# Transposing the normalised A of six batches by DMA instead of on TensorE, and E's way through DRAM on SP's queue

## The chip, the cores and the metric

One of the eight cores of a Trainium2 chip runs the program. TensorE multiplies matrices (PE; its weight loads are shown as PEld), VectorE (DVE), ScalarE (ACT) and GpSimd (POOL) do the rest of the arithmetic, and SyncE (SP) issues DMAs. Each engine runs its own list of instructions in order and waits on semaphores for the others. The metric is the time of one execution on the device in microseconds.

## What is computed

A Nyström attention (8 batches, 8 heads, 576 positions, 64 per head, 32 landmarks) feeds a multiplicative feed-forward layer:

```python
q_lm = q.reshape(B, H, m, S // m, D).mean(axis=3)       # m = 32 landmarks of 18 rows
k_lm = k.reshape(B, H, m, S // m, D).mean(axis=3)
A  = softmax(scale * q @ k_lm^T)                         # 576 x 32 per head
Bm = softmax(scale * q_lm @ k_lm^T)                      # 32 x 32
C  = softmax(scale * q_lm @ k^T)                         # 32 x 576
Z  = Bm^T / (norm_1(Bm) * norm_inf(Bm) + 1e-6)
for _ in range(6):
    Z = 2 * Z - Z @ Bm @ Z
x = (A @ Z @ C @ v), heads put side by side              # 4608 x 512
out = ((x @ w1) * (x @ w2) @ w3) @ w_out                 # 4608 x 512
```

## The kernel before

Nothing is multiplied in the order written above. `w3 @ w_out` is made once at the start (`w34`, the w3 rows j = 0 to 7, each in two f16 parts of the weights). Four heads of one batch are a quad: there are 16 quads, n = 0 to 15, and quad n belongs to batch n // 2. For each quad the landmarks' means are taken (on PE for the first `NE` quads, on POOL for the others), the scores S and A are multiplied (`s_mm`, `a_mm`), and softmaxes are taken. The exponentials of C, named E, have to be turned so that positions lie on partitions: for the first `NT` = 4 quads by PE, for later ones by DVE in 32x32 blocks (`ecx`), a write to DRAM (`edr`, one DMA a batch, `e_out`) and eight reads back (`ecT`, `e_move`). Then C v is multiplied (`cv_mm`, tasks C0 to C7), the inverse Z is iterated for two batches at a time, and Z C v is folded into w1 and w2 (`W`, then `U`, whose results are `u`).

A's softmax, normalised, is written by POOL to `ah` (`a_norm`, L744). PE turns it in blocks of 128x128 (`a_trans`, L753): four blocks a quad, and a fifth for the odd quads that holds the last two rows of each landmark for both quads. ACT copies the blocks from PSUM into `aT` (`a_copy`, L763 for the four, L766 for the fifth) and sorts the columns as it does so. `aT` is the moving operand of `d1_mm`, which makes both halves of the feed-forward layer in tiles of 192 positions; ACT copies one half out (`asb`, L1097), DVE multiplies it by the other into `ab` (L1103), and `d2_mm` multiplies `ab` with `w34`. ACT scales the result into `osb` (L1129), and SP stores it (`d2_store`, L1144) in the order of rows that `aT`'s columns stand for.

The order of each engine's list is made before anything runs, by a planner in the file (`Plan`). Every task is added with an engine, a duration, the tasks it depends on, the buffers it takes and gives back, and a priority (a due time); the planner plays the program through with these and writes the instructions in the order it found. On PE the constants `MP`, `MT` and `MY` favour staying in the same kind of matmul (full array, or one of several tilings). DMAs are issued in the planned order too: the loads of q and k, of w1 and w2, and the six writes and 48 reads of E from POOL, everything else from SP (the last three stores partly from ACT). A DMA on a queue in this program waits for the one eight places earlier.

In the code nearly all matmuls go through one helper, so they have one line, L296, and are told apart by the tiles that they write and read.

Of the kernel before, what the change touches and what calls it, by code (L numbers as in the profile page):

```python
# [15 lines left out]
S = 576  # L16
# [3 lines left out]
GRP = S // M  # L20
# [1 line left out]
DM = 512  # L22
DF = 1024
HALF = 288
MP = 1.8
MT = 6.0
MY = 0.0
GR = int(2.0)
THIRD = 192
NCH = 8  # L30
# [3 lines left out]
NV = 4  # L34
# [179 lines left out]
def kernel(  # L214
# [93 lines left out]
    def dense(b):  # L308
        return T0 + PER * b
# [7 lines left out]
        return max(12.0 + 6.0 * n, first)  # L317

    def lane(g):
        return dense(GROUPS[g][0]) - 22.0  # L320

    def cvt(b):
        g, i = GOF[b]
        return lane(g) - 10.0 + 3.0 * (i + 2 - len(GROUPS[g]))

    LQ = int(1.0)
    NT = 2 * int(2.0)
    NE = int(2.0)
    L0 = 3.0
    UO = 2.0  # L330
    GO = 10.0


    def const_a():
# [133 lines left out]
                                 scale=1.0 / (WSC * WSC))  # L468
        return fn

    W1 = 2.0
    JS = int(4.0)
    JH = 3.0
    PWL = [(), (3,), (1, 4), (1, 3, 5), (1, 3, 5, 7)][int(2.0)]
    PEB = int(2.0)
    FIRST = [(0, 1), (1, 4), (4, 8)] if PEB else [(0, 4), (4, 8)]

    def w34_tasks():
        for j in range(8):
            p0 = 4.0 + 7.7 * j  # L480
            add(f"w3n{j}", "SP", 0.43 if j < PEB else 1.7, load_w3(j), acq=[("w3n", f"w3n{j}", 1, 3 if j == 0 and PEB else 2)],
                prio=-0.01 if j == 0 else 0.1 + 0.01 * W1 - 0.005 if j == 1 else p0 - 7.0,
                after=0.0 if j < 2 else max(0.0, p0 - 7.0 - 4.0), parts=1 if j < PEB else 4, move=1.42 if j < PEB else 1.8,
                lat=1.9, share=3.75 if j < PEB else 2.85)
            if j == 0:
                for c in range(8):
                    if c % 2 == 0:
                        add(f"wf{c}", "SP", 1.72, load_wout(c), prio=0.1 + 0.01 * c, parts=4, move=1.55, lat=1.9, share=1.92)
                    add(f"woh{c}", "ACT", 0.53, wout_hi(c), deps=[f"wf{c - c % 2}"],
                        prio=1.0 + 0.1 * c)  # L490
                    if c in PWL:
                        add(f"ws{c}", "ACT", 0.53, wout_scale(c), deps=[f"wf{c - c % 2}", f"woh{c}"], prio=1.05 + 0.1 * c)
                        add(f"wol{c}", "POOL", 1.05, wout_sub(c), deps=[f"ws{c}"], prio=-1.0 + 0.1 * c)
                    else:
                        add(f"wol{c}", "DVE", 0.62, wout_lo(c), deps=[f"wf{c - c % 2}", f"woh{c}"],
                             prio=1.0 + 0.1 * c)
            cuts = FIRST if j == 0 else [(0, 4), (4, 8)]
            for h, (c0, c1) in enumerate(cuts):
                k = (c1 - c0) / 4
                deps = [f"w3n{j}"] + ([f"wt{j}{h - 1}"] if h else [])  # L500
                pe = j < PEB
                add(f"wt{j}{h}", "PE" if pe else "DVE", 0.86 * k + 0.03 if pe else 0.64,
                    (w3_ptr if pe else lambda j, h, c0, c1: w3_tr(j, h))(j, h, c0, c1), deps=deps + ["cb"],
                    acq=[("P", f"ptr{j}{h}", 1, 2)], rel=[f"w3n{j}"], prio=p0 - 4.0 + h, mode="128x32" if pe else None)
                add(f"wh{j}{h}", "ACT", 0.13 + 0.35 * k, w3_hi(j, h, c0, c1), deps=[f"wt{j}{h}"] + ([f"wh{j}0"] if h else []),
                    acq=[] if h else [(f"w3t{W3S[j]}", f"w3t{j}", 1, 8)] + ([(f"vb{W3S[j]}", f"wv{j}", 1, 1)] if W3S[j] > 1 else []), rel=[f"ptr{j}{h}"], prio=p0 - 3.5 + h)
                add(f"wl{j}{h}", "DVE", 0.1 + 0.5 * k, w3_lo(j, h, c0, c1), deps=[f"wh{j}{h}"], rel=[f"ptr{j}{h}"],
                    prio=p0 - 3.5 + h)
            part = {c: h for h, (c0, c1) in enumerate(cuts) for c in range(c0, c1)}
            for c in range(8):  # L510
                last = [f"wv{j}"] if c == 7 and W3S[j] > 1 else []
                hi, lo = [f"woh{c}", f"wh{j}{part[c]}"], [f"wol{c}", f"wl{j}{part[c]}"]
                bank1 = [("P", f"pw{j}", 1, 1)] if c == 0 else []
                if j < JS:
                    add(f"mh{j}{c}", "PE", 0.22, w34_mm(j, c, 0), deps=hi + ([f"mh{j}{c - 1}"] if c else []),
                        acq=bank1, prio=p0 + 0.7 * c - JH, mode="full")
                    add(f"mm{j}{c}", "PE", 0.435, w34_mm(j, c, 1), deps=lo + [f"mh{j}{c}"] + ([f"mm{j}{c - 1}"] if c else []),
                        rel=[f"w3t{j}"] + last, prio=p0 + 0.7 * c, mode="full")
                    continue
                add(f"mm{j}{c}", "PE", 0.65, w34_mm(j, c), deps=hi + lo + ([f"mm{j}{c - 1}"] if c else []),  # L520
                    acq=bank1, rel=[f"w3t{j}"] + last, prio=p0 + 0.7 * c, mode="full")
            add(f"wo{j}", "ACT", 0.48, w34_out(j), deps=[f"mm{j}7"], rel=[f"pw{j}"], prio=p0 + 6.0)
# [168 lines left out]
    def a_mm(n):  # L691
        def fn():
            T, lm, ps, o = Tqs[at(f"Tq{n}")], lmTs[at(f"lmT{n}")], a_bank(n), 4 if n % 2 else 2
            for i in range(4):
                for e in range(2):
                    mm(ps[:, 128 * i:128 * i + 128], T[:, o + 4 * i:o + 4 * i + 4, :, e], lm[:, 4:8, :, e],
                       start=(e == 0), stop=(e == 1))
        return fn

# [41 lines left out]
    def a_norm(n):  # L741
# [4 lines left out]
                in1=tinies[at(f"ta{n}")][:, 0:g].unsqueeze(2).to_broadcast([128, g, M]), op=ALU.mult)  # L746
        return fn

    def a_trans(n):
        def fn():  # L750
            ps = bank(at(f"pT{n}")).bitcast(FP16)
            for i in range(a_cols(n) // 128):
                nc.tensor.transpose(  # L753
                    out=ps[:, 128 * i:128 * i + 128],
                    in_=ahs[at(f"ah{n}")][:, 4 * i:4 * i + 4, :].rearrange("p g m -> p (g m)"),
                    identity=ident16[:, :])
        return fn

    def a_copy(n):
        def fn():  # L760
            b, qd = divmod(n, 2)
            ps, t = bank(at(f"pT{n}")).bitcast(FP16), aTs[at(f"aT{b}")]
            nc.scalar.copy(out=t[:, qd, 0:512].rearrange("p (i l r) -> p i l r", i=4, r=4),  # L763
                           in_=ps[:, 0:512].rearrange("p (i r l) -> p i l r", i=4, r=4))
            if qd:
                nc.scalar.copy(out=t[:, :, 512:S].rearrange("p a (l r) -> p a l r", r=2),  # L766
                               in_=ps[:, 512:640].rearrange("p (a r l) -> p a l r", a=2, r=2))
        return fn

    def quad_tasks(n):  # L770
# [2 lines left out]
        add(f"lq{n}", "POOL", 1.2, load_qk(n), acq=[("nat", f"nat{n}", 1, 3)],  # L773
            prio=p - (16.0 if n < 4 else 20.0),
            after=max(L0, p - (20.0 if n < 4 else 20.0)), parts=2, move=3.3, lat=1.83, share=4.46)
        add(f"lv{n}", "SP", 1.72, load_v(n), acq=[(f"vb{n % NV}", f"vb{n}", 1, 1)], deps=["ce"] + ([f"mm{n}7"] if W3S[n] > 1 else []) if n < 4 else [], prio=cvt(b) - 5.0 + qd, after=max(12.0, cvt(b) - 5.0 - 3.0 + 3 * qd), parts=4, move=2.05, lat=1.9, share=1.57)
        loads = [f"lq{n}"]
        add(f"tk{n}", "DVE", 0.77, trans(n, 1), deps=loads, acq=[("Tk", f"Tk{n}", 1, 1)],
            rel=[f"nat{n}"], prio=p - 3.0)
# [47 lines left out]
        else:  # L827
# [7 lines left out]
            rel=[f"pA{n}"], prio=p + 0.7)  # L835
        add(f"ae{n}", "ACT", 0.63 if qd else 0.53, a_exp(n), deps=[f"as{n}"], prio=p + 3.0)
        add(f"au{n}", "DVE", 1.03 if qd else 0.9, a_sum(n), deps=[f"ae{n}"], prio=p + 4.0)
        add(f"an{n}", "POOL", 1.3 if qd else 1.05, a_norm(n), deps=[f"au{n}"], acq=[("ah", f"ah{n}", 1, 1)],
            rel=[f"ea{n}", f"ta{n}"], prio=p + 5.0)
        add(f"tA{n}", "PE", 0.36 if qd else 0.29, a_trans(n), deps=[f"an{n}", "cd"],  # L840
            acq=[("P", f"pT{n}", 1, 1)], rel=[f"ah{n}"], prio=p + 9.0, mode="full")
        add(f"aT{n}", "ACT", 0.65 if qd else 0.48, a_copy(n), deps=[f"tA{n}"] + ([f"aT{n - 1}"] if qd else []),
            acq=[] if qd else [("aT", f"aT{b}", 1, 24)], rel=[f"pT{n}"], prio=p + 9.5)


    def cv_mm(b):
# [286 lines left out]
    def d2_store(t, f0=0, f1=DM, part=None, eng=nc.sync):  # L1133
        def fn():
            k = 0
            o_sb = osb[at(f"os{t}")]
            p0 = 0
            while p0 < 128:
                b, x = divmod(128 * t + p0, S)
                i, u = divmod(x, 128)  # L1140
                n = 4 if i < 4 else 2
                w = min(128 - p0, 32 * n - u)
                if part in (None, k):
                    eng.dma_start(  # L1144
                        out=out[S * b:S * b + S, :].rearrange("(l r) f -> l r f", r=GRP)[
                            u // n:(u + w) // n, 4 * i:4 * i + n, f0:f1],
                        in_=o_sb[p0:p0 + w, f0:f1])
                p0, k = p0 + w, k + 1
        return fn

# [3 lines left out]
    def dense_tasks():  # L1154
        for k in range(3 * B):
            b, th = divmod(k, 3)
            for j in range(8):
                p = dense(b) + PER * (8 * th + j) / 24.0
                deps = [f"aT{2 * b}", f"aT{2 * b + 1}"]
                deps += [f"uo{b}{wi}{j // 4}{qd}" for wi in range(2) for qd in range(2)]  # L1160
                add(f"d{b}{j}{th}", "PE", 0.33, d1_mm(b, j, th), deps=deps + ["wo7"],
                    acq=[("P", f"pD{b}{j}{th}", 1, 1)],
# [102 lines left out]
```

## Time and profile before

| | us |
|---|---|
| median of 3 runs | 271.1 |
| lowest, highest | 269.78, 271.92 |
| the profiled execution, device time | 271.5 |
| its span in the profile | 269.7 |

| engine | busy us | share of the span |
|---|---|---|
| PE | 255.3 | 95% |
| ACT | 191.9 | 71% |
| DVE | 188.8 | 70% |
| POOL | 151.1 | 56% |

The granted TensorE clock was full (0.999). The profile shows one execution. A group of instructions is named by its line, engine, operation and tiles (`out<-in`, buffer numbers left out), with a count and a duration. A matmul's duration there includes the time for its last column to come out of the array, so back-to-back matmuls follow each other faster than their durations say: the stretch that a row of them takes, divided by their number, is what one costs. Idle time has the name of what ended it. The chain of waits goes back from the last instruction to whatever released each step, and shows what the end of the program hung on.

### The profile page before, as it was taken

What the parts mean: (1) busy time and instruction counts of PE and PEld (TensorE: products, weight loads), DVE (VectorE), ACT (ScalarE), POOL (GpSimd) and SP (SyncE); (2) the same over time, 40 slices, a digit from 0 to 9 for tenths busy, and PEclk for the clock granted to TensorE, in tenths of its full rate; (3) what the DMA queues carried; (4) which work ended last, traced back from release to release, by engine and by line L of the source; (5) the groups of instructions that cost most, each with busy time, mean ns of one, the idle gap of its engine ahead of it and who ended that gap; (6) DMA issues with size and microseconds to landing.
All of it is one profiled execution on the core that took longest, in us unless ns stands there. A gap on an engine that the chain in (4) does not pass through costs nothing.

```text
span 269.7 us, 9632 instructions
## 1 busy us (share of the span) xinstructions
PE 255.3 (95%) x3848; PEld 165.7 (61%) x3848; DVE 188.8 (70%) x519; ACT 191.9 (71%) x558; POOL 151.1 (56%) x199
## 2 busy tenths in 40 slices
PE   3998899999999989999999999999999999999993
PEld 3663455654547746666577577666766765765762
DVE  2489999899796989489779976866953561641530
ACT  3656957467589769568978798788677548659651
POOL 8427959799989996978989957711080000000000
PEclk9999999999999999999999999999999999999999
DMA  7999999999995494998797948512351121222123
GB/s 228 258 256 251 245 261 212 270 263 235 193 216 120 122 205 84 257 267 264 160 183 195 262 145 270 132 61 78 126 141 46 41 80 39 80 78 81 43 79 117
DMA packets 29518, 44.80 MB, mean 166 GB/s; under 512 B 4129, under 2 KB 18081, under 8 KB 29473
## 3 DMA queue, kind: packets, MB, share of 16 engines
q0 software_dynamic: 9568, 19.01, 34.3%
q1 hardware_dynamic: 19664, 24.91, 31.5%
q8 instruction: 30, 0.49, 0.8%
q10 hardware_dynamic: 240, 0.26, 0.3%
q14 instruction: 16, 0.12, 0.2%
HBM read 42.34 MB, written 13.37 MB: 207 GB/s over the span
## 4 chain that ended last, share of the span: by engine, by line
PE 82%; ACT 8%; DVE 5%; issue 2%; POOL 1%; ACTq 0%; DVEq 0%; POOLq 0%
PE bank L296 75%; PE wide L296 5%; ACT u L1014 3%; DVE wo L399 2%; PE bank L753 1%; ACT ec L637 1%; ACT asb L1097 1%; ACT lmT L603 1%; ACT osb L1129 1%; ACT w L467 1%; PE wide L645 1%; DVE tiny L622 1%; DVE Tq L558 1%; ACT aT L763 0%; DVE Tk L558 0%
## 5 line engine op out<-in xcount | busy, mean ns | idle before, releaser
L296 PEld LDWEIGHTS <-u 128*128 128x128 f16 x960 | 80.6, 98 | 35.1 <-issue 7.4
L1103 DVE TENSOR_TENSOR ab<-asb,bank 128x192 f16<-128x192 f16 x192 | 58.8, 346 | 37.0 <-ACT asb L1097 36.5
L296 PE MATMUL bank<-aT,u 128*128 128x192 f16 x768 | 77.2, 246 | 0.8 <-DVE ab L1103 0.3
L296 PE MATMUL bank<-w,ab 128*128 128x512 f16 (+1 forms) x296 | 73.1, 374 | 0.0
L1097 ACT CAST asb<-bank 128x192 f16<-128x192 f32 x192 | 56.0, 338 | 16.5 <-PE bank L296 15.8
L296 PE MATMUL bank<-wo,u 128*128 128x512 f16 x192 | 48.2, 380 | 2.3 <-DVE wo L399 1.3
L573 POOL TENSOR_TENSOR ls<-ls 128x128 f32<-128x128 f32 (+2 forms) x56 | 41.6, 742 | 3.6
L296 PEld LDWEIGHTS <-ab 128*128 128x128 f16 x296 | 26.6, 98 | 22.2 <-issue 3.9
L1014 ACT CAST u<-bank 128x512 f16<-128x512 f32 x64 | 34.4, 604 | 3.8 <-PE bank L296 3.6
L566 POOL TENSOR_TENSOR ls<-nat 128x1152 f32<-128x1152 f16 x14 | 33.3, 2376 | 4.9 <-ACT lm L580 3.6
L744 POOL TENSOR_TENSOR ah<-ea,tiny 128x512 f16<-128x512 f32 (+1 forms) x16 | 18.5, 1160 | 23.5 <-DVE tiny L738 8.7
L1129 ACT ACTIVATE osb<-bank 128x512 f32<-128x512 f32 x35 | 21.4, 610 | 13.5 <-PE bank L296 11.6
L680 POOL DMA_DIRECT2D ecT<-edr x48 | 26.4, 562 | 0.8 <-PE bank L296 0.7
L603 ACT COPY lmT<-lmu 32x128 f16<-32x128 f16 x64 | 18.8, 294 | 5.0 <-DVE lmu L594 3.4
L296 PE MATMUL bank<-w,wT 64*32 64x512 f16 x512 | 19.0, 380 | 0.9 <-issue 0.9
L296 PEld LDWEIGHTS bank<-xz 32*32 32x32 f32 x768 | 11.2, 105 | 8.9 <-issue 3.5
L296 PE MATMUL bank<-xz 32*32 32x64 f32 (+1 forms) x768 | 15.1, 213 | 1.0 <-issue 0.6
L450 DVE SCALAR_TENSOR_TENSOR u<-bank,u 128x512 f16<-128x512 f32 (+2 forms) x17 | 10.6, 644 | 6.2 <-ACT u L444 6.2
L622 DVE TENSOR_REDUCE tiny<-wide 128x1 f32<-128x576 f32 x16 | 12.0, 752 | 3.3 <-PE wide L296 2.7
L444 ACT ACTIVATE u<-bank 128x512 f16<-128x512 f32 (+2 forms) x17 | 9.6, 573 | 5.1 <-PE bank L296 5.1
L296 PEld LDWEIGHTS <-Tq 128*128 128x128 f16 x160 | 10.6, 97 | 4.1 <-issue 0.2
L558 DVE STREAM_TRANSPOSE Tk<-nat 128x448 f32<-128x448 f32 (+1 forms) x32 | 13.0, 443 | 0.0
(100 smaller groups left out, 322.9 us busy)
## 6 DMA issues: line engine op xcount, KB each, us to landing
vb<-in_v_dram SPq DMA_DIRECT2D x32, 160.0 KB, 6.5
out_dram<-osb SPq DMA_DIRECT2D x37, 128.0 KB, 2.3
nat<-in_k_dram POOLq DMA_DIRECT2D x16, 288.0 KB, 5.9
nat<-in_q_dram POOLq DMA_DIRECT2D x16, 288.0 KB, 7.6
vb<-in_v_dram SPq DMA_DIRECT2D x32, 128.0 KB, 6.7
out_dram<-osb SPq DMA_DIRECT2D x16, 256.0 KB, 2.9
edr<-ecx POOLq DMA_DIRECT2D x6, 640.0 KB, 4.9
w3n<-in_moe_w_dram SPq DMA_DIRECT2D x16, 128.0 KB, 7.5
```

What stands on the lines that cost most here:

```text
L296: nc.tensor.matmul(out_, lhsT, rhs, start=start, stop=stop, **({} if pos is None else {"tile_position": pos}))
L558: nc.vector.transpose(out=T[:, to:to + r1 - r0].rearrange("p r l e -> p (r l e)").bitcast(FP32), in_=nats[at(f"nat{n}")][:, t, r0:r1].rear ...
L566: nc.gpsimd.tensor_tensor(out=l, in0=nat[:, :, 0:9, :], in1=nat[:, :, 9:18, :], op=ALU.add)
L573: nc.gpsimd.tensor_tensor(out=l[:, :, x:x + m, :], in0=l[:, :, x:x + m, :], in1=l[:, :, y:y + m, :], op=ALU.add)
L603: nc.scalar.copy(out=lm[r, :, h, :], in_=u[r].rearrange("p t l e -> p t (l e)"))
L622: nc.vector.reduce_max(out=mx[:, 0:1], in_=s_cols(), axis=AX.X)
L680: (nc.gpsimd if LQ else nc.sync).dma_start(out=ecTall[32 * x:32 * x + 32, i + q_, :, 0:w, :].rearrange("p h c l -> p h (c l)"), in_=src[:, ...
L744: nc.gpsimd.tensor_tensor(out=ahs[at(f"ah{n}")][:, 0:g, :], in0=eas[at(f"ea{n}")][:, 0:g, :], in1=tinies[at(f"ta{n}")][:, 0:g].unsqueeze(2 ...
L1014: nc.scalar.copy(out=uu[at(f"u{b}{qd}")][:, wi, 512 * half:512 * half + 512], in_=bank(at(f"pU{b}{wi}{half}{qd}")))
L1097: nc.scalar.copy(out=asb[at(f"as{b}{j}{th}")], in_=bank(at(f"pD{b}{j}{th}"))[:, 0:THIRD])
L1103: nc.vector.tensor_mul(ab[:, j, c0:c0 + THIRD], asb[at(f"as{b}{j}{th}")], bank(at(f"pD{b}{j}{th}"))[:, THIRD:2 * THIRD])
L1129: nc.scalar.activation(out=osb[at(f"os{t}")], in_=bank(at(f"pE{t}")), func=AXF.Copy, scale=2.0 ** -12)
```

## The change

For batches 2 to 7 (`b >= NA`, with `NA` = 2) the four 128x128 blocks of a quad are turned by one DMA from `ah` to `aT`, issued by SP. PE keeps the fifth block of the odd quads, and ACT its copy. Since the DMA can't sort columns, the rows are sorted when A is multiplied: block i takes the landmarks u*4 + i (u = 0 to 7) of all 16 rows r, so that the weights are loaded from `Tq` with a step of eight elements where it was two; the stores put each row where it belongs. E's write and reads are issued by SP instead of POOL (`LQ` = 0). Quad 1's mean is taken on POOL instead of PE (`NE` = 1). Of the eight chunks of w_out, POOL subtracts chunk 3 instead of chunks 1 and 4 (`PWL`), after a scaling on ACT; DVE does the others. Further constants of the planner change, and with them every engine's order.

```diff
-MP = 1.8
+MP = 2.1
-MY = 0.0
+MY = 1.0
...
     def lane(g):
-        return dense(GROUPS[g][0]) - 22.0
+        return dense(GROUPS[g][0]) - 24.0
...
-    LQ = int(1.0)
+    LQ = int(0.0)
     NT = 2 * int(2.0)
-    NE = int(2.0)
+    NE = int(1.0)
+    NA = int(2.0)
     L0 = 3.0
-    UO = 2.0
-    GO = 10.0
+    UO = 3.0
+    GO = 8.0
...
-    W1 = 2.0
+    W1 = 3.0
...
-    PWL = [(), (3,), (1, 4), (1, 3, 5), (1, 3, 5, 7)][int(2.0)]
+    PWL = [(), (3,), (1, 4), (1, 3, 5), (1, 3, 5, 7)][int(1.0)]
...
     def a_mm(n):
         def fn():
             T, lm, ps, o = Tqs[at(f"Tq{n}")], lmTs[at(f"lmT{n}")], a_bank(n), 4 if n % 2 else 2
+            by = T[:, o:o + 16].rearrange("p (i r) l e -> p i (r l) e", i=4)
+            if n // 2 >= NA:
+                by = T[:, o:o + 16].rearrange("p r (u i) e -> p i (r u) e", i=4)
             for i in range(4):
                 for e in range(2):
-                    mm(ps[:, 128 * i:128 * i + 128], T[:, o + 4 * i:o + 4 * i + 4, :, e], lm[:, 4:8, :, e],
+                    mm(ps[:, 128 * i:128 * i + 128], by[:, i, :, e], lm[:, 4:8, :, e],
                        start=(e == 0), stop=(e == 1))
...
+    def a_move(n):
+        def fn():
+            b, qd = divmod(n, 2)
+            nc.sync.dma_start_transpose(
+                out=aTs[at(f"aT{b}")][:, qd, 0:512].rearrange("p (i m) -> p i m", i=4),
+                in_=ahs[at(f"ah{n}")][:, 0:16, :].rearrange("p g m -> p (g m)"))
+        return fn
+
     def a_trans(n):
         def fn():
             ps = bank(at(f"pT{n}")).bitcast(FP16)
-            for i in range(a_cols(n) // 128):
+            for i in range(4 if n // 2 >= NA else 0, a_cols(n) // 128):
...
-            nc.scalar.copy(out=t[:, qd, 0:512].rearrange("p (i l r) -> p i l r", i=4, r=4),
-                           in_=ps[:, 0:512].rearrange("p (i r l) -> p i l r", i=4, r=4))
+            if b < NA:
+                nc.scalar.copy(out=t[:, qd, 0:512].rearrange("p (i l r) -> p i l r", i=4, r=4),
+                               in_=ps[:, 0:512].rearrange("p (i r l) -> p i l r", i=4, r=4))
...
+        if b >= NA:
+            add(f"tx{n}", "SP", 1.33, a_move(n), deps=[f"an{n}"] + ([f"tx{n - 1}"] if qd else []),
+                acq=[] if qd else [("aT", f"aT{b}", 1, 24)], rel=[f"ah{n}"], prio=p + 9.0, move=0.75, lat=1.9, share=0.5)
+            if qd:
+                add(f"tA{n}", "PE", 0.07, a_trans(n), deps=[f"an{n}", "cd"], acq=[("P", f"pT{n}", 1, 1)],
+                    rel=[f"ah{n}"], prio=p + 9.0, mode="full")
+                add(f"aT{n}", "ACT", 0.18, a_copy(n), deps=[f"tA{n}", f"tx{n - 1}"], rel=[f"pT{n}"], prio=p + 9.5)
+        else:
...
+                rows = out[S * b:S * b + S, :]
+                if i < 4 and b >= NA:
+                    rows = rows.rearrange("(u i r) f -> i r u f", u=8, i=4)[i, u // 8:(u + w) // 8, :, f0:f1]
+                else:
+                    rows = rows.rearrange("(l r) f -> l r f", r=GRP)[u // n:(u + w) // n, 4 * i:4 * i + n, f0:f1]
                 if part in (None, k):
-                    eng.dma_start(
-                        out=out[S * b:S * b + S, :].rearrange("(l r) f -> l r f", r=GRP)[
-                            u // n:(u + w) // n, 4 * i:4 * i + n, f0:f1],
-                        in_=o_sb[p0:p0 + w, f0:f1])
+                    eng.dma_start(out=rows, in_=o_sb[p0:p0 + w, f0:f1])
...
-                deps = [f"aT{2 * b}", f"aT{2 * b + 1}"]
+                deps = [f"aT{2 * b + 1}"] + ([f"aT{2 * b}"] if b < NA else [f"tx{2 * b}", f"tx{2 * b + 1}"])
```

In SP's new list, batch 3's eight reads of E stand behind the transposing DMA of quad 7 and three stores, batch 5's behind a store and the DMA of quad 11, and batch 7's behind one store; batch 3's write stands behind the DMA of quad 6.

More of the change, by code (lines that the diff above doesn't have):

```diff
@@ L481, in w34_tasks @@
             add(f"w3n{j}", "SP", 0.43 if j < PEB else 1.7, load_w3(j), acq=[("w3n", f"w3n{j}", 1, 3 if j == 0 and PEB else 2)],
-                prio=-0.01 if j == 0 else 0.1 + 0.01 * W1 - 0.005 if j == 1 else p0 - 7.0,
-                after=0.0 if j < 2 else max(0.0, p0 - 7.0 - 4.0), parts=1 if j < PEB else 4, move=1.42 if j < PEB else 1.8,
+                prio=-0.01 if j == 0 else 0.1 + 0.01 * W1 - 0.005 if j == 1 else p0 - 9.0,
+                after=0.0 if j < 2 else max(0.0, p0 - 9.0 - 4.0), parts=1 if j < PEB else 4, move=1.42 if j < PEB else 1.8,
                 lat=1.9, share=3.75 if j < PEB else 2.85)
@@ L775, in quad_tasks @@
             after=max(L0, p - (20.0 if n < 4 else 20.0)), parts=2, move=3.3, lat=1.83, share=4.46)
-        add(f"lv{n}", "SP", 1.72, load_v(n), acq=[(f"vb{n % NV}", f"vb{n}", 1, 1)], deps=["ce"] + ([f"mm{n}7"] if W3S[n] > 1 else []) if n < 4 else [], prio=cvt(b) - 5.0 + qd, after=max(12.0, cvt(b) - 5.0 - 3.0 + 3 * qd), parts=4, move=2.05, lat=1.9, share=1.57)
+        add(f"lv{n}", "SP", 1.72, load_v(n), acq=[(f"vb{n % NV}", f"vb{n}", 1, 1)], deps=["ce"] + ([f"mm{n}7"] if W3S[n] > 1 else []) if n < 4 else [], prio=cvt(b) - 4.0 + qd, after=max(12.0, cvt(b) - 4.0 - 3.0 + 3 * qd), parts=4, move=2.05, lat=1.9, share=1.57)
         loads = [f"lq{n}"]
@@ L837, in quad_tasks @@
         add(f"au{n}", "DVE", 1.03 if qd else 0.9, a_sum(n), deps=[f"ae{n}"], prio=p + 4.0)
-        add(f"an{n}", "POOL", 1.3 if qd else 1.05, a_norm(n), deps=[f"au{n}"], acq=[("ah", f"ah{n}", 1, 1)],
+        add(f"an{n}", "POOL", 1.3 if qd else 1.05, a_norm(n), deps=[f"au{n}"], acq=[("ah", f"ah{n}", 1, 2 if qd and b >= NA else 1)],
             rel=[f"ea{n}", f"ta{n}"], prio=p + 5.0)
[L840 to L843, printed above, removed]
+        if b >= NA:
[6 more added lines that the diff above has]
+        else:
+            add(f"tA{n}", "PE", 0.36 if qd else 0.29, a_trans(n), deps=[f"an{n}", "cd"],
+                acq=[("P", f"pT{n}", 1, 1)], rel=[f"ah{n}"], prio=p + 9.0, mode="full")
+            add(f"aT{n}", "ACT", 0.65 if qd else 0.48, a_copy(n), deps=[f"tA{n}"] + ([f"aT{n - 1}"] if qd else []),
+                acq=[] if qd else [("aT", f"aT{b}", 1, 24)], rel=[f"pT{n}"], prio=p + 9.5)
     def cv_mm(b):
```

## The prediction

> **What bounds the kernel now.** I read the page's engine totals first, then its shares of the chain of waits, then who waits for whom with PE (the TensorE matmuls) as the waiter.
>
> ```profile
> PE 255.3 (95%) x3848; PEld 165.7 (61%) x3848; DVE 188.8 (70%) x519; ACT 191.9 (71%) x558; POOL 151.1 (56%) x199
> ...
> PE 82%; ACT 8%; DVE 5%; issue 2%; POOL 1%; ACTq 0%; DVEq 0%; POOLq 0%
> ```
>
> ```profile
> PE bank L296 <- POOL lmT L355: 4.5, 1, 4.5
> PE bank L296 <- issue: 1.5, 2, 0.9
> PE bank L296 <- DVE wo L399: 1.3, 2, 0.7
> PE bank L296 <- ACT u L444: 1.0, 1, 1.0
> PE bank L296 <- DVE ab L1103: 0.6, 2, 0.4
> ```
>
> The columns of the second are total us, times and the longest. PE is the bound: apart from 4.5 us before its first matmul and some 6 us after its last, it stands still for about 5 us, most of that between 24.8 and 30.2 us, where the weight product waits for DVE and ACT. From 31 us on, what PE no longer has to do comes off the end, unless a new wait takes its place. So I price PE work first and look for waits second.
>
> **Base.** The profiled execution took 271.5 us by the device's clock: its span of 269.7 and 1.8 around it. The median of the three runs is 271.1. The sum is made on 271.5.
>
> **Transposes leave PE.** Twelve quads lose four transposes each (n = 4 to 15); the odd ones keep their fifth. The chain in order of time (start, us, what) gives the price, and two other rows I need:
>
> ```profile
> 47.78 0.44 PE wide L645 x4
> ...
> 71.77 0.22 PE bank L753 x4
> ...
> 82.22 0.49 ACT aT L763
> ...
> 89.96 0.46 PE wide L296 x8
> ...
> 133.33 0.67 ACT aT L763
> ```
>
> Four take 0.22 us, so 48 take 48 x 0.055 = 2.7 us, all in the stretch where PE is the bound: **-2.7 us**.
>
> **Copies leave ACT.** Twelve copies at L763 of about 0.60 us, 7.2 us of ACT's 191.9. ACT isn't the bound, but the chain passes through L763 at 82 and 133 us, 0.49 + 0.67 = 1.16 us. Others queue on ACT there (u and asb copies), so part of it will be taken by the next: between 0 and -1.2, I take half, **-0.6 us**.
>
> **The twelve transposing DMAs.** None is in this trace. One moves a tile of 128x512 f16, 128 KB. Nearest is a store of 128 KB, then E's write of 640 KB:
>
> ```profile
> out_dram<-osb SPq DMA_DIRECT2D x37, 128.0 KB, 2.3
> ...
> edr<-ecx POOLq DMA_DIRECT2D x6, 640.0 KB, 4.9
> ...
> ecT<-edr POOLq DMA_DIRECT2D x24, 80.0 KB, 3.2
> ```
>
> Landing in 2.3 to 4.9 us, against 1 us or so for transpose and copy. Who needs it? The timeline has the last piece of batch 6's aT and the first product that reads it:
>
> ```profile
> 181.92 0.33 ACT L766 COPY aT<-bank 128x128 f16<-128x128 f16 x1
> ```
>
> ```profile
> 227.69 1.49 PE L296 MATMUL bank<-aT,u 128*128 128x192 f16 x16
> ```
>
> 45 us lie between, and 48 for batch 2. The attention part runs that far ahead, so the landing is covered: 0. If that cover were gone, each batch would pay the landing, 6 x 2.3 to 4.9 = 14 to 29 us. On SP's queue the transpose waits for POOL's normalisation, and v loads, E's transfers and stores queue behind it; that is a rival below.
>
> **E moves from POOL's queue to SP's.** 54 issues of 0.55 us (L680) leave POOL, 30 us; POOL isn't waited for by PE after its start, so 0. SP pays 0.43 (the v loads, L541) to 0.55 us (the stores, L1144) for each: 23 to 30 us more, and the twelve transposes 5 to 16 if one costs one to three issues, on the 161 issues, some 75 us, that it makes now. 121 us of 270 bounds nothing by amount; its order is the rival's matter.
>
> **Quad 1's mean goes from PE to POOL.** 18 matmuls, 18 x 0.056 = 1.0 us, but at 18.2 us, before PE's idle stretch at 24.8 to 30.2: PE would only wait longer there. Between 0 and -1.0; I take 0. POOL gets 2.36 + 3.15 = 5.5 us instead, from about 17.7 us when quad 1's q lands, where it is idle until 21.8; quad 2's mean starts 1.4 us later, and its scores stand on PE at 37.6, 9 us after that mean ended: 0.
>
> **The w_out split.** DVE subtracts chunks 1 and 4 (POOL did) and POOL chunk 3. Chunk 1 comes at about 8 us, where DVE is idle; chunk 2 comes early too, now that its load stands ahead of w3's second. Behind 12.8 us DVE keeps five: 0, with a rival below.
>
> **Weight loads at a wider step.** For six batches the 96 loads of Tq read every eighth element (16 bytes) instead of every second (4). Eight load-and-multiply pairs take 0.46 us, 57 ns each. Upper bound: the four-byte transposes at L645, 0.44/4 = 110 ns. 96 x 53 ns = 5.0 us at worst. Loads of consecutive (u) and every-second elements (Tq) both take 97 to 98 ns in the page, so I take 0.
>
> **Stores and order.** SBUF-side rows stay 2 KB; only rows in DRAM are scattered. The last store is as large as before: 0, bound +0.5. The changed constants reorder everything: counted in both orders, PE changes 109 times between full-array and tiled matmuls in each, so there is no term; either of the "issue" waits (0.9) or DVE's (0.6) may go or come again.
>
> **Sum:** 271.5 - 2.7 - 0.6 = **268.2 us**, 1.2% less. Its own range: down to 271.5 - 2.7 - 1.2 - 1.0 - 0.6 = 266.0, and up to 271.5 - 2.7 + 0.9 = 269.7.
>
> **Rival 1, E comes late (slower).** PE runs in order and each C V product is put where E lands. Now: batch 7's last read was issued at 200.8 us and landed within 3.6, and PE reads it at 205.0: 0.6 to spare. Batch 3: 100.9 + 5.5 against 107.0, 0.6; batch 5: 154.0 + 5.4 against 159.3, none; batch 2: 2.4; batches 4 and 6 over 6. On POOL the reads followed short arithmetic. On SP they stand behind stores and transposes that wait for others:
>
> ```profile
> SPq L1144 <- ACT asb L1097: 94.5, 22, 8.6
> ```
>
> 22 waits of 4.3 us on average. Against it: E's write needs 4.9 us to land anyway, which hides waits up to there, and eight reads at 0.43 instead of 0.55 save 1 us. With 2.5 us late, PE waits 1.9 + 2.5 + 1.9 + 0.1 = 6.4 us: **274.6**. It uses up the gain of 3.3 from 1.5 us late (0.9 + 1.5 + 0.9). The Trainium skill (VectorE: DVE Perf Modes, The three transpose paths) gives 1309 ns for a 128x128 transpose by DMA against 390 on TensorE; four in a row would be an estimated 5.2 us of queue per quad, which would bring this case nearer; no run here shows it yet.
>
> **Rival 2, the wide step costs.** The 5.0 us bound in full: **273.2**; by half, 270.7. It decides as soon as a load outlasts the 53 ns matmul beside it. For it: nothing in the trace. Against it: 2-byte and 4-byte steps cost the same. The Trainium skill (Advanced Engine Details and Errata, SBUF Cachelines) says that reads want two hits in each 16-byte line, which the new step never gives; by that rule this rival would be the forecast. No load in this trace has such a step.
>
> **Rival 3, DVE slows at the start.** The subtraction at L399 takes 0.69 us alone, but beside POOL's sums far longer:
>
> ```profile
> 14.17 1.25 DVE L399 SCALAR_TENSOR_TENSOR wo<-ecT,wo 128x512 f16<-128x512 f32 x2
> ...
> 23.07 3.33 DVE L399 SCALAR_TENSOR_TENSOR wo<-u,wo 128x512 f16<-128x512 f32 x2
> ```
>
> ```profile
> 21.81 2.37 POOL L566 TENSOR_TENSOR ls<-nat 128x1152 f32<-128x1152 f16 x1 [1.29 <-DMA nat<-in_q_dram]
> 24.26 3.81 POOL L573 TENSOR_TENSOR ls<-ls 128x512 f32<-128x512 f32 x4
> ```
>
> Quad 1's mean now fills POOL from 17.7 on, so chunks 4 and 5 could be hit as well: 2 x (1.70 - 0.69) = 2.0 us on DVE, which PE waits for there: **270.2**.
>
> **Rival 4, nothing comes of it:** the freed PE time becomes waits for ACT and DVE, both about 70% busy: **271.3**. Against it: PE's waits after 31 us are small now.
>
> **Chances.** Forecast 0.54, rival 1 0.22, rival 2 0.10, rival 3 0.08, rival 4 0.06. Within 1% of 271.5 (2.7 us) is about what this kernel's measurement can't tell from no change. Faster by over 1%: most of the forecast, 0.47. Slower by over 1%: rival 1 nearly whole, and more than one mishap, 0.23. Within: the rest, 0.30. The range runs from 266.0 over rivals 2 to 4 to 275.0, which leaves out the later half of rival 1.
>
> **What would show it.** PE's transposes at 24 instead of 72 and PE busy down by some 3 to 4 us; ACT down 7, POOL down about 25; no wait of PE for a DMA of ecT or aT (one would be rival 1); Tq's loads still at 97 ns and their pairs at 57 (rival 2); L399 over 1 us only twice (rival 3). The forecast is wrong if PE's idle time past 31 us grows by more than 2 us.

## The result, and the profile after

| | before | after |
|---|---|---|
| median, us | 271.5 | 281.4 |
| lowest, highest | 269.78, 272.76 | 280.33, 286.01 |
| ratio after to before, 95% interval | | 1.0356 [1.0263, 1.045] |
| the profiled execution, device time | 271.5 | 286.0 |
| its span | 269.7 | 284.0 |

The kernel is 3.6% slower. I had forecast 268.2 and at most 275.0. The profile after is of the longest of its four executions, and the ratios here and below leave out every execution that lies more than 1.5% above the fastest of its kernel, as this one does, while the medians keep them. First the page's engine totals and its shares of the chain of waits:

```profile
PE 255.8 (90%) x3782; PEld 164.8 (58%) x3782; DVE 192.1 (68%) x520; ACT 186.2 (66%) x545; POOL 125.6 (44%) x149
...
PE 53%; DMA 16%; DVE 14%; ACT 7%; SPq 3%; POOL 3%; issue 3%; DVEq 0%; ACTq 0%; POOLq 0%
```

PE issues 66 matmuls fewer (48 transposes, 18 of the mean) and is still busy as long; its share fell from 95 to 90%, and PE's part of the chain from 82 to 53%. The missing parts went to DMA and DVE. Who waits for whom, with PE as the waiter (total us, times, longest):

```profile
PE bank L296 <- DMA osb<-in_moe_w_dram: 5.4, 2, 4.6
PE bank L296 <- ACT w L468: 3.1, 1, 3.1
PE bank L296 <- ACT aT L779: 2.7, 2, 2.3
PE bank L296 <- issue: 2.2, 1, 2.2
PE bank L296 <- DVE ab L1124: 2.2, 4, 1.1
...
PE bank L296 <- DMA ecT<-edr: 0.6, 1, 0.6
```

Of the first row, 4.6 us lie ahead of the first matmul, where it was 4.5 before under another name. The two rows below it are new, and E, my chief rival, is the last. The windows of those two waits and of the 3.4 us behind each show why PE's busy time didn't fall (columns: window and length, then busy us and count of PE, PEld, DVE, ACT and POOL, granted clock, DMA share, GB/s):

```profile
84.40:90.20 5.80, 2.03 (x28) 1.69 (x21) 2.16 (x4) 2.50 (x9) 4.86 (x5) 1.00 1.09 267
90.20:93.60 3.40, 2.99 (x19) 2.75 (x19) 2.84 (x9) 3.13 (x12) 2.62 (x5) 0.50 1.05 195
161.00:165.30 4.30, 2.04 (x80) 0.76 (x62) 1.58 (x5) 1.86 (x6) 0.00 (x0) 1.00 0.62 115
165.30:168.70 3.40, 3.40 (x22) 2.00 (x15) 1.39 (x5) 2.74 (x9) 0.00 (x0) 0.50 0.73 181
```

In the two stretches ahead PE was busy for 35 and 47% of the time, and in the 3.4 us behind each its clock was granted at half, so that up to 1.7 us are lost on top of the wait. The trace of after has three of these before the end (at 32, 90 and 165 us), that of before none. Not every wait brings one: from 108.4 to 111.7 us PE was busy for 32%, and the clock stayed full. By the Trainium skill (TensorE: Matmul & The Clock Gate, Part 1) the clock is halved after an idle window of 3413 ns; the length of the half-clock stretches agrees, but no single wait of PE was that long here once it had begun: the longest is 3.13 us.

The two waits have different origins. The one at 88 us, in the timelines of DVE, ACT and PE (start, us, work, then idle time and what ended it):

```profile
86.21 0.78 DVE L559 STREAM_TRANSPOSE Tq<-nat 128x576 f32<-128x576 f32 x1 [2.90 <-DMA nat<-in_q_dram]
86.92 0.72 DVE L623 TENSOR_REDUCE tiny<-wide 128x1 f32<-128x576 f32 x1
```

```profile
87.67 0.19 ACT L630 COPY bsc<-wide 128x32 f32<-128x32 f32 x1 [3.42 <-DVE tiny L623]
87.75 0.60 ACT L468 ACTIVATE w<-bank 128x512 f16<-128x512 f32 x1
```

```profile
88.40 1.15 PE L296 MATMUL bank<-aT,u 128*128 128x192 f16 x12 [3.13 <-ACT w L468]
```

Quad 8's q (issued at 76.1) lands at 86.2; DVE stands before it, with quad 6's score maximum behind it in its list; ACT waits for the maximum with L468 behind that; PE waits for the bank that L468 frees. Nobody needed quad 8's q yet. The one at 163 us:

```profile
163.44 0.27 ACT L779 COPY aT<-bank 128x128 f16<-128x128 f16 x1 [2.83 <-DMA aT<-ah]
```

L779 is the copy of the fifth block. It writes columns of both quads of the batch in one instruction, and so waits for the transposing DMA of its own odd quad, which was issued 5.5 us earlier (157.89). The plan had it wait for the even quad's alone. Before, this copy followed a PE transpose.

On SP, the waits of the transposing DMA, and what SP issued from 48 to 80 us:

```profile
SPq L756 <- POOL ah L748: 22.8, 2, 20.9
```

```profile
48.40 2.45 SPq L542 DMA_DIRECT2D vb<-in_v_dram  x3
72.00 2.18 SPq L756 DMA_TRANSPOSE aT<-ah  x1
74.28 1.98 SPq L542 DMA_DIRECT2D vb<-in_v_dram  x4
```

Quad 4's transposing DMA waits 20.9 us for POOL, and the v loads of quads 5 to 7 stand behind it. Before, they were issued from 49.8 us on.

### The profile page after: what moved, and what is told of

Its sections match the earlier page's. It is cut to its first block, busy times and chain, and to the rows that moved or that the text cites. A ratio compares the mean times of both kernels' runs of the same rounds, so it can differ in the third digit from the quotient of the medians.

```text
span 284.0 us, 9486 instructions
## 1 busy us (share of the span) xinstructions
PE 255.8 (90%) x3782; PEld 164.8 (58%) x3782; DVE 192.1 (68%) x520; ACT 186.2 (66%) x545; POOL 125.6 (44%) x149
## 4 chain that ended last, share of the span: by engine, by line
PE 53%; DMA 16%; DVE 14%; ACT 7%; SPq 3%; POOL 3%; issue 3%; DVEq 0%; ACTq 0%; POOLq 0%
PE bank L296 49%; DMA edr<-ecx 5%; DMA u<-in_moe_w_out_dram 4%; DMA nat<-in_q_dram 4%; DMA aT<-ah 3%; PE wide L296 2%; DVE ab L1124 2%; SPq L681 2%; DMA ecT<-in_moe_w_out_dram 1%; DVE wo L400 1%; POOL ls L567 1%; DVE bank L911 1%; ACT ec L638 1%; DVE Tk L559 1%; DVE tiny L623 1%
## 5 line engine op out<-in xcount | busy, mean ns | idle before, releaser
L296 PEld LDWEIGHTS <-u 128*128 128x128 f16 x960 | 83.0, 99 | 47.3 <-issue 17.7
L296 PE MATMUL bank<-aT,u 128*128 128x192 f16 x768 | 82.2, 250 | 5.7 <-ACT w L468 3.1
L296 PE MATMUL bank<-w,ab 128*128 128x512 f16 (+1 forms) x296 | 74.3, 377 | 0.1
L1118 ACT CAST asb<-bank 128x192 f16<-128x192 f32 x192 | 57.3, 330 | 20.9 <-PE bank L296 18.2
L567 POOL TENSOR_TENSOR ls<-nat 128x1152 f32<-128x1152 f16 x15 | 35.6, 2374 | 37.0 <-ACT lm L581 24.9
L574 POOL TENSOR_TENSOR ls<-ls 128x128 f32<-128x128 f32 (+2 forms) x60 | 44.5, 741 | 4.2
L1035 ACT CAST u<-bank 128x512 f16<-128x512 f32 x64 | 35.7, 612 | 3.0 <-PE bank L296 2.9
L559 DVE STREAM_TRANSPOSE Tq<-nat 128x576 f32<-128x576 f32 (+2 forms) x24 | 12.5, 546 | 2.9 <-DMA nat<-in_q_dram 2.9
L296 PEld LDWEIGHTS <-Tq 128*128 128x128 f16 x160 | 11.8, 126 | 3.1 <-issue 0.8
L296 PEld LDWEIGHTS <-wT 64*32 64x32 f16 x512 | 5.6, 89 | 12.9 <-issue 10.5
```

The source lines that it names most:

```text
L296: nc.tensor.matmul(out_, lhsT, rhs, start=start, stop=stop, **({} if pos is None else {"tile_position": pos}))
L559: nc.vector.transpose(out=T[:, to:to + r1 - r0].rearrange("p r l e -> p (r l e)").bitcast(FP32), in_=nats[at(f"nat{n}")][:, t, r0:r1].rear ...
L567: nc.gpsimd.tensor_tensor(out=l, in0=nat[:, :, 0:9, :], in1=nat[:, :, 9:18, :], op=ALU.add)
L574: nc.gpsimd.tensor_tensor(out=l[:, :, x:x + m, :], in0=l[:, :, x:x + m, :], in1=l[:, :, y:y + m, :], op=ALU.add)
L1035: nc.scalar.copy(out=uu[at(f"u{b}{qd}")][:, wi, 512 * half:512 * half + 512], in_=bank(at(f"pU{b}{wi}{half}{qd}")))
L1118: nc.scalar.copy(out=asb[at(f"as{b}{j}{th}")], in_=bank(at(f"pD{b}{j}{th}"))[:, 0:THIRD])
```

## The experiments

Times are medians; a ratio is to the kernel before, run on the same chip, with its 95% interval. Medians of different jobs are compared by these ratios, since the kernel before itself had medians from 271.0 to 273.6.

**The copy that waits.** e1 cuts the copy in two in the kernel after; e5 and e6 put the DMAs alone into the kernel before, without and with the cut.

```diff
-            if qd:
+            if qd and b >= NA:
+                for a in range(2):
+                    nc.scalar.copy(out=t[:, a, 512:S].rearrange("p (l r) -> p l r", r=2),
+                                   in_=ps[:, 512 + 64 * a:576 + 64 * a].rearrange("p (r l) -> p l r", r=2))
+            elif qd:
```

> The changed kernel with the copy of the fifth block (L779) cut into two, one for each quad of the batch, order kept. Theory W (ACT's copy stands behind the transposing DMA of its own quad, because one copy over both quads spans the columns that the DMA writes; ACT runs in order, so PE runs out of PSUM banks, and an idle PE loses half its clock for 3.4 us): no wait of ACT for a DMA of aT is left (5.2 us in two waits now), PE's waits for that copy go (2.7 us), and so does the half-clock stretch at 165 us (1.7 us): 3 to 5 us less than the changed kernel's 281.4, some 277. Rival Q (SP's queue and the transfers set the pace, the copy only waits where ACT would wait anyway): 280 to 282.

> Only the transposing DMAs (and what belongs to them: the wider step, the stores' rows) are put into the kernel before; quad 1's mean, the w_out split, E's queue and every constant stay as before. Theory W (the DMAs take 2.7 us from PE, as forecast, and give 3 to 4 us back at the one copy of the fifth block that waits for its quad's DMA): 271 to 273 us, with waits of ACT's copy for a DMA of aT and of PE for that copy. Theory D (the DMAs themselves cost: their small packets delay the loads of q and E): 277 us or more, with PE late behind q loads. If my forecast for this part was right all the same: 268 us.

> The same, with the copy of the fifth block cut in two, so that each half writes columns of one quad only. Theory W: 268 to 269.5 us (before less 2.7 for 48 transposes, less 0 to 1.2 of copies, plus 0.5 for the wider step), below the kernel before. Theory D: still 274 us or more, and the split is worth under 1 us here.

e1: 277.95 us, 1.0239 [1.0164, 1.0314], as expected; PE's wait for this copy, and the copy's for a DMA, are gone. e5: 286.53, 1.0564 [1.0486, 1.0643], far above both what my forecast for this part and theory W said. Theory D has the number, but not its waits: PE waits for this copy there, and only 0.2 us for q. e6: 282.02, 1.0309 [1.0183, 1.0435], above 274 as theory D had it, but with the copy worth more than the 1 us that D left it. e5 and e6 have the same order on every engine but for the cut copy. So the copy is real, about 1.2% in one order (the intervals overlap) and 2.5% in the other (they don't), and it isn't all: the DMAs alone, in the order that the planner made with them and no other edit, cost 3% with the copy mended. In e5 the waits of the copy, and of PE for it, are on the page's list:

```profile
PE bank L296 <- ACT aT L779: 8.0, 4, 3.7
...
ACT aT L779 <- DMA aT<-ah: 12.2, 5, 4.3
```

**The rest of the change.** e7 takes the DMAs out of the kernel after (`NA` = 8); e8 puts E back on POOL's queue (`LQ` = 1); e3 undoes the start (`NE` = 2, `PWL` index 2, `W1` = 2, w3's priority with -7).

> The kernel after with all of A's transposes back on PE and their copies on ACT, and the rest of the change kept (quad 1's mean on POOL, E on SP's queue, the new constants). If the loss lies in the start and the order (theory S): 279 to 281 us, as the 2.7 us of transposes come back and the 3.5 us of the copy's wait go. If it lies in the transposing DMAs (theory D): 272 to 274 us.

> The kernel after with E's write and reads back on POOL's queue, nothing else. By the waits shown (PE for ecT 0.6 us) E's queue is worth 0 to 1 us: 280 to 282 us. If E's transfers on SP's queue are what holds up the loads of v and the transposing DMAs behind them: 276 us or less, and the waits of ACT's copy for the DMA shrink.

> The changed kernel with the constants of the start as before: quad 1's mean on PE, chunks 1 and 4 of w_out on POOL, order of the first loads as before. Theory S (DVE's subtractions at 18 us take 2 us each beside POOL's mean, and the second w3 row comes later: PE's waits for DVE and ACT up to 31 us, and a half-clock stretch at 32 us): C v of batch 0 begins at 39.5 as before instead of 41.7, of batch 1 at 51 instead of 55.5, no half-clock stretch before 40 us, 3 to 4 us less, some 278. Rival: what is lost at the start is slack that later waits take up: 280 to 282.

e7: 273.63, 1.0089 [1.0048, 1.0129], as theory D had it. Everything but the transposing DMAs is worth +0.9%, and the DMAs, for all the work that they take from PE, another 2.6% (1.0356 / 1.0089). These two parts go by e7's own order, since `NA` is a constant of the planner as well, and each engine's list in e7 differs from that of the kernel after. e8: 301.54, 1.1078 [1.0971, 1.1185]; e3: 287.57, 1.0601 [1.0519, 1.0682]. Both missed, because a constant of the planner changes the engines' lists: e3's start is as early as before's (C v of batch 0 at 39.7 us), and new stalls of PE follow at 48, 86 and 109 us, with 10.5 us of waiting for the copy of the fifth block; in e8 ACT's fifth-block copies wait for DMAs of aT 26.7 us in all, where they wait 5.2 in the kernel after. So neither prices the queue or the start by itself; e7 has both, with an order of its own, at 0.9%, in which a loss and a gain may have met. From here on the experiments move single entries of the lists and leave the constants alone.

**The v loads behind the DMA.** e2 puts the loads of quads 5 to 7 ahead of quad 4's DMA on SP; e4 does that together with e1's and e3's edits.

```diff
+    early = [t for t in order if t.name in ("lv5", "lv6", "lv7")]
+    order = [t for t in order if t not in early]
+    place = {t.name: i for i, t in enumerate(order)}
+    place = max(place["lv4"], place["C1"]) + 1
+    order[place:place] = early
```

> The changed kernel with the v loads of quads 5, 6 and 7 ahead of quad 4's transposing DMA on SP, nothing else moved. Theory B (that DMA waits 21 us for POOL and holds 12 loads back, which then land in the stretch where q and k of later quads and w1, w2 are loaded; quad 7's q lands after 10 us, DVE waits for it, then ACT, then PE): the waits of PE at 85 to 91 us (3.1 and 1.1 us) and the half-clock stretch that follows (1.7 us) go, 4 to 6 us less, some 276. Rival V (the transfers are slow because there is more to move: transposing in small packets, E's reads on one queue): the wait stays, 280 to 282.

> All three of these together. If the three losses are separate they add: 10 to 14 us less, 267 to 271, and the 2.7 us of transposes that left PE begin to show against the kernel before. If they share one cause (SP's queue), 274 or more.

e2: 278.99, and no interval could be given: three executions lie from 278.8 to 279.3, one at 273.5. In its profile, of 279.2 us, the stall at 84 us stayed: PE waits 3.0 us for L468. (The q that comes late is quad 8's, not quad 7's as the expectation has it.) e4: 279.17, 1.0251 [1.0171, 1.0331], not the 267 to 271 of three losses that add up; since e3's constants reorder it, it doesn't price the loads. So in this order nothing speaks for the theory that the held v loads make quad 8's q late, and e16 below, with four executions that agree, decides against it. e14 and e15 below take the same question up where the loads of four quads are held.

**The turning itself.** While the packets of quad 11's transposing DMA ran in the kernel after, from 160.30 to 162.54 us, little else moved (windows as above; the last column is GB/s):

```profile
156.30:160.30 4.00, 4.00 (x78) 2.32 (x76) 3.69 (x14) 3.07 (x10) 3.84 (x5) 1.00 0.71 279
160.30:162.55 2.25, 1.19 (x24) 0.45 (x22) 0.95 (x4) 0.30 (x1) 0.60 (x2) 1.00 1.19 76
```

From 279 to 76 GB/s. It is the extreme of the twelve: in nine of them, this one included, all queues together moved 76 to 166 GB/s after 141 to 279 in the 4 us ahead, and in the last three 201 to 220, more than ahead of them. This led to controls in which the DMAs carry the same bytes without turning them: e10 and e11 are e6 with plain DMAs (the four arithmetic engines' orders are the same), e12 is the kernel after with them. In e13, e6 with `NA` = 6, only the last two batches are turned by DMA.

```diff
-            nc.sync.dma_start_transpose(
-                out=aTs[at(f"aT{b}")][:, qd, 0:512].rearrange("p (i m) -> p i m", i=4),
+            nc.sync.dma_start(
+                out=aTs[at(f"aT{b}")][:, qd, 0:512],
                 in_=ahs[at(f"ah{n}")][:, 0:16, :].rearrange("p g m -> p (g m)"))
```

> The kernel with only the DMAs added and the copy split, where each transposing DMA is a plain one: the same 128 KB between the same tiles, at the same place of every list, in rows of 1 KB and without turning them (so what stands in aT is A unturned, and the output is not the reference's). Theory D (the transposing form holds up the other transfers: while its packets run, all queues together move 74 to 200 GB/s where 200 to 290 is moved else): 268 to 271 us, 11 us less. Theory S (SP's place in the order, its wait for POOL's normalisation and what queues behind it): 280 to 283 us, no change.

> The same with two plain DMAs of 64 KB for each, in rows of 256 bytes, the size of the transposing DMA's packets, so 512 packets a quad and nearly the same time of issue on SP (the output is not the reference's either). If the small packets are the cost: as with the transposing DMAs, 279 us or more. If the turning itself is: 269 to 272 us, as with rows of 1 KB.

> The kernel after with a plain DMA of 1 KB rows in place of each transposing one and nothing else changed, the one copy of the fifth block included (A stays unturned). Theory D: the copy's wait shrinks with the landing (5 us to about 2) and the half-clock stretches at 90 and 165 us go: 271 to 274 us, which is the kernel after with its transposes on PE (273.6), less up to 2.7. If order and waits on SP are the loss: 279 us or more.

> The kernel before with only batches 6 and 7 turned by DMA and the copy split: these four DMAs run past 185 us, where the DMA engines are half idle. Theory D (collisions cost): no loss there, and 16 x 0.055 = 0.9 us of transposes and some copies gained: 269 to 271 us, same as before or 0.3 to 0.7% below. If a transposing DMA costs wherever it stands: 273 us or more.

e10: 279.44, 1.0356 [1.0249, 1.0464], no better than e6's 1.0309. e11: 278.86 (273.84 to 286.0), no interval. e12: 277.52, 1.0252 [1.0155, 1.0348] against 1.0356 with turning, between its two forecasts. Its plain DMA of quad 11 has the same fall, from 297 to 139 GB/s, so the fall isn't peculiar to the turning. e13: 274.46, 1.0108 [0.9993, 1.0222], which holds all from no loss to 2% and answers nothing. Theory D, that the turning form is the cost, fell by its own numbers: 268 to 271 was expected of e10.

**The place on SP.** In e6 quad 4's DMA stands ahead of the v loads of all four quads 4 to 7. What SP issues from 40 to 80 us in e6:

```profile
40.31 4.75 SPq L390 DMA_DIRECT2D w3n<-in_moe_w_dram  x8
65.30 1.31 SPq L756 DMA_TRANSPOSE aT<-ah  x1
66.72 13.34 SPq L542 DMA_DIRECT2D vb<-in_v_dram  x14
```

20 us of nothing, and then v loads in the stretch in which the others load. e14 moves that one DMA behind the loads; e15 does so with plain DMAs; e16 is e1 with e2's edit.

```diff
+    tx4 = [t for t in order if t.name == "tx4"][0]
+    order.remove(tx4)
+    order.insert([t.name for t in order].index("lv7") + 1, tx4)
```

> The kernel with only the DMAs added and the copy split (282.0 us), with one thing moved: on SP, quad 4's transposing DMA stands behind the v loads of quads 4 to 7 instead of ahead of them, where it held them from 45 to 67 us. Theory S (held loads fall into the busiest stretch for the DMA engines and make q, E and instructions late): 273 to 277 us. If only the turning and not the place counts: 280 us or more.

> The same with plain DMAs of 1 KB rows in place of the transposing ones (A stays unturned). If place, copy and turning are all of the loss: 268 to 270 us, the sum that I forecast. If something else is left, for example SP's later waits or the order of PE: 273 us or more.

> The kernel after with both small edits: the copy split, and the v loads of quads 5 to 7 ahead of quad 4's transposing DMA on SP. If the two add up: 273 to 276 us (281.4 less 3.5 and 3 to 5). If they share one cause: 277 to 279 us.

e14: 279.1, 1.0164 [1.0024, 1.0304] against e6's 1.0309, within the intervals and between its two forecasts. e15: 277.6, 1.009 [0.9952, 1.0229], against 1.0356 [1.0249, 1.0464] of e10, which differs in this one place alone: the intervals don't touch. The place of a single DMA in SP's list is worth some 2.6% there by the ratios. They rest on few numbers: two executions enter e15's, and all four of it (273.3 to 279.3 us) overlap e10's (278.1 to 281.4). And something is left in e15, where 268 to 270 was expected if nothing were. The same stretch of e15:

```profile
46.24 12.90 SPq L542 DMA_DIRECT2D vb<-in_v_dram  x16
65.88 0.57 SPq L756 DMA_DIRECT2D aT<-ah  x1
```

Of PE's waits in e6, the one for E (2.6 us at 97, C v of batch 2) is in neither e14's list nor e15's:

```profile
PE bank L296 <- DMA edr<-ecx: 2.6, 1, 2.6
```

But e10 doesn't have it either. What e10 has, and e15 lacks, are these, and two half-clock stretches, at 115 and 169 us:

```profile
PE bank L296 <- issue: 3.4, 3, 2.9
PE bank L296 <- DVE Tq L559: 2.2, 1, 2.2
```

So the place pays by other waits in each pair, and how it leads to each of them is not shown.

e16: 279.62, 1.0272 [1.0181, 1.0363], where e1 alone has 1.0239: in the order of the kernel after, the same remedy does nothing, and PE still waits 3.3 us for L468.

**DVE's place in line.** In the kernel after, DVE's transposes of quad 8's q stand ahead of quad 6's score maximum; in the kernel before, in e6 and in e7 behind it. e18 is e1 with this edit, e19 adds e2's, and e20 is e18 with plain DMAs.

```diff
+    held = [t for t in order if t.name in ('tq8', 'tk8')]
+    order = [t for t in order if t not in held]
+    place = [t.name for t in order].index("f020") + 1
+    order[place:place] = held
```

> The kernel after with the copy split (278.0 us, 1.024 of before), where DVE's transposes of quad 8's q and k stand behind quad 6's score maximum and three ab products instead of ahead of them; the instructions of the other engines keep their order. If DVE's place in line is the stall at 80 us: PE's wait for L468's w (3.3 us) and for the next ab (1.1) and the half clock behind them (up to 3.4) go: 270 to 273 us. If the wait only moves to the next reader of q: 276 us or more.

> The same with the v loads of quads 5 to 7 ahead of quad 4's transposing DMA on SP as well. If held loads make q late in this order too: 1 to 3 us below the one before it, 268 to 271. If in this order they cost nothing, as the pair without DVE's edit showed: the same time within 1 us.

> The copy split, DVE's transposes of quad 8 late, and plain DMAs of 1 KB rows for the transposing ones (A stays unturned). If the four parts (copy, DVE's place, turning, and the 2.4 of the rest of the change) make up the whole: 269 to 271 us, by 273.6 with the transposes on PE less 2.7 and a little. If something is left: 273 us or more.

e18: 276.64, 1.0199 [1.0129, 1.0269], above what I expected; from e1's 1.0239 the step is within the intervals. The profile shows the step all the same: L468 is no longer among PE's waits (3.5 us in e1), and there is no half-clock stretch before the end (6.8 us at 86 in e1). e19: 274.0, 1.0083 [1.0041, 1.0126]; the intervals of e18 and e19 don't touch. So the early v loads, worth nothing in e16, are worth 1.2% once DVE doesn't hold the same stretch back. e20: 274.24, 1.0106 [1.003, 1.0182]; turning against not turning is again within the intervals.

With three small edits (the copy, DVE's list, SP's list) the kernel is at 1.0083, as fast as with the transposes on PE (1.0089). No version beat the kernel before.

## Why the prediction was wrong

**What held.** PE lost the 48 transposes (24 are left of 72), ACT lost 5.7 us and POOL 25.5. Between e7 and e19, which differ in the DMAs and the edits that undo their waits, PE's busy time falls from 253.4 to 251.2 us: 2.2, my 2.7 less what the wide step costs. In the kernel after PE waited for E for 0.6 us in all, so rival 1's own price (6.4 us of waiting) wasn't paid. E's place on SP isn't free of traces, though: its writes make up 5% of the chain of waits, and quad 15's DMA, whose data POOL had ready at 210.1 us, stood behind batch 7's eight reads and was issued at 213.3.

**The step that failed: "The twelve transposing DMAs ... so the landing is covered: 0".** I asked who needs the data, found `d1` 45 us later, and stopped there. Landing was wider than I had bounded it (2.2 to 7.1 us from issue, by the packets' times; I had 2.3 to 4.9), but far inside the 45 us. Two others stood behind the DMAs. One is ACT's copy of the fifth block, an instruction in the diff, which writes into the same tile: about 1.2%, some 3 us, in the kernel after (e1), within the intervals, and 2.5% in before's order (e5 to e6). The other is what is queued behind SP's wait for POOL. I named the v loads in that sentence and then priced E alone: rival 1 had the right queue and the wrong passenger. The loads cost 1.2% in the mended order of the kernel after (e18 to e19) and some 2.6% in before's order (e10 to e15).

**"The changed constants reorder everything ... so there is no term".** I compared the number of changes of mode on PE. The term was on DVE: one transpose that waits for a load, placed ahead of a maximum that was ready. It cost PE 3.1 + 1.1 us in the profile, and the half clock behind that; in time it is 0.4% (e1 to e18), within the intervals, and the loads' 1.2% with it. It takes the constants and the DMAs together: e7 has the constants alone and e6 the DMAs alone, and neither has this order.

**What a wait costs.** In the base and in the rivals each wait stood at its own length. Three half-clock stretches add up to 3 x 1.7 = 5.1 us in the profiled execution; by the mean clocks of the other three (0.981 to 0.984, where it has 0.977) I estimate about two such stretches there.

**Quad 1's mean and w_out, "0".** By the mark that I had set, rival 3 did not come: still only two of DVE's subtractions take over 1 us, together 4.00 where it was 3.33 before. In the chain in order of time (start, us, what):

```profile
18.31 4.00 DVE wo L400 x2
```

They come at 18 instead of 23 us, though, and C v of batch 0 begins at 41.7 instead of 39.5. That the start's constants cause this is not shown: e7 has them too, with 3.46 us for the two subtractions at 17.6, and its C v of batch 0 begins at 38.8, that of batch 1 at 52.6 (50.8 before). All of the change but the DMAs costs 0.9%, 2.4 us (e7); how much of it is the start and how much E's queue or the order, e3 and e8 could not separate.

**Rival 2, the wide step.** Loads of Tq, all together with their duration in ns (min/median/max), in the kernel after and in e7:

```profile
L296 PEld LDWEIGHTS <-Tq x160: 96/143/168, 22.6 to 204.6; 128*128 128x128 f16 x160
```

```profile
L296 PEld LDWEIGHTS <-Tq x160: 96/97/100, 21.3 to 194.5; 128*128 128x128 f16 x160
```

The median load is longer by about half with the wider step. By the Trainium skill (Advanced Engine Details and Errata, SBUF Cachelines) a read that hits another cacheline each time pays a penalty, whose size it doesn't give; the trace agrees. But the loads overlap the matmuls: eight pairs take 0.50 us in the chain instead of 0.46, so all twelve quads pay 0.5 us, not 5.0. The condition that I had set, a load that outlasts the matmul beside it, said nothing: a load took 97 ns before too, in a pair of 57. (That a transposing DMA can't sort the columns itself, the reason for the step, no run here tests.)

**Rival 4** is the last piece. The 2.2 us that PE gains don't reach the end even in e19: PE waits there 3.4 us for DVE's `ab`, where it waits 0.7 in e7. These are the totals, e7's first:

```profile
PE bank L296 <- DVE ab L1124: 0.7, 2, 0.4
```

```profile
PE bank L296 <- DVE ab L1128: 3.4, 5, 1.2
```

Whether that wait is only the next in line or comes from DVE's moved transposes was not tried.

**What is left.** From the forecast (0.988 of before) to 1.0356 there are 4.8%. The three edits of e19 take back 2.7 (1.0356 to 1.0083). The remaining 2 are about what e7's 0.9 and the 1.2 of gain that I forecast make together; which waits eat that gain, beyond the one for `ab`, is open. Also open: the turning form against a plain DMA (e6/e10, after/e12, e14/e15, e18/e20) favours the plain one in three of four pairs by 0.7 to 1%, each within the intervals.

## What to carry to other kernels

When a transfer replaces an engine's work, its reader is only the first to ask after: list every instruction that writes the same tile or buffer, and everything behind the new wait on the queue that issues it, and price the earliest of them. In a kernel with in-order engines near a full PE, look for the ready instruction behind one that waits for a load, in each engine's list. A cause can be real and its removal show nothing while a second holds the same stretch (e16 against e19), so remove them in pairs before one is called nothing.

## What the runs showed of the hardware

- The granted clock fell to 0.50 for 3.4 us three times in the kernel after, behind stretches of 3.9 to 5.8 us in which PE was busy for 35 to 53%, and for 6.8 us in e1 behind a wait of 3.5; a stretch of 3.3 us with PE busy for 32% brought none. Each 3.4 us cost up to 1.7.
- A transposing DMA's 512 packets of 256 bytes ran for 0.8 to 2.7 us in the kernel after, while all queues together moved 76 to 220 GB/s. SP took a median of 1.23 us to issue one, against 0.52 for a plain one in e12. The Trainium skill (Advanced Engine Details and Errata, X-Bar Transpose (TRN2)) has such DMAs as fast as regular ones: the packets of the last three took 0.81 to 0.97 us, those of e12's last three plain ones of the same 128 KB 0.70 to 0.86, which nearly agrees, and the kernel's time agrees as far as the pairs can tell; the time of issue does not.
- PE's wait for "issue" of 2.2 us in the kernel after ends at 111.7 us, 2.2 us after a packet of 16 KB on the instruction queue (109.5); e6, e10 and e11 have waits of 2.0 to 2.9 us beside such packets, the kernel before one of 0.9. That the fetch is their cause was not tested.
